# The second token product of a filter-and-mixer kernel in seven products of 256 columns, from the second batch on, with the earlier form of the first batch's filter step

## The chip, the cores and the metric

One core of a Trainium2 chip runs the whole kernel. The time is device microseconds for one execution, as a median of several runs. Before the change it is 2583.15 us (three runs, 2580.81 to 2583.3); the profiled execution has a span of 2581.1 us.

## The reference: what is computed

Eight batches of x (3008 positions, 256 channels, float32) pass two blocks.

```python
X = np.fft.rfft(x, axis=1)                          # gfnet_mixing
x = np.fft.irfft(X * (filt_r + 1j * filt_i), n=3008, axis=1)

h = np.maximum(x.T @ w_tok1, 0.0) @ w_tok2          # token products: 3008 -> 256 -> 3008, per batch
u = x + h.T
h2 = np.maximum(u @ w_ch1, 0.0) @ w_ch2             # channel products: 256 -> 1536 -> 256
out = u + h2
```

The weights arrive as float64, so every piece of them is converted to float32 on the chip once ("conversion" below).

## The kernel before

The Fourier transforms are matrix products with tables. A batch's positions are split as 64 x 47; the first half of the transform is written to DRAM (z_tmp), the middle (32 steps, one for each k) does the second half, the filter and the first half of the inverse, and writes g_tmp; the last half of the inverse is added inside the same PSUM sums as the second token product.

The mixer goes through 8 batches, 6 tiles of 512 positions each (the last 448), and 6 steps `jp` for each tile: 288 items. An item runs the two channel products for a sixth of the hidden width. They are already done in the seven-product form: a 2 x 2 block product with 7 multiplications of 256 columns in place of 8, at the price of sums on VectorE (DVE). The filter of the batches to come runs in between, one or two of its steps for each item.

```python
def u_unit(b, m, h1, ut, dh):            # second token product + last half of the inverse transform
    w = width(m)                         # 512, or 448 for m = 5
    ps = bank(free_bank())
    for t in range(TC):                  # TC = 2
        nc.tensor.matmul(ps[:, 0:w], h1[:, t, ts(dh, P)], w2[:, t, ds(m * 512, w)], start=(t == 0), stop=False)
    for q in range(4):                   # 128 columns each
        ...
        nc.tensor.matmul(ps[:, ds(q * P, n)], t4[b, c][:, r, ts(dh, P)], wai[:, 0:n], start=False, stop=(q == 3))
    nc.scalar.copy(out=ut[:, dh, 0:w], in_=ps[:, 0:w])

def mix(next_ready):
    ...
    for i in range(len(items) + 1):
        ...
        s = up_first(...); up_middle(...)        # 4 of the 7 products; ACT copy, 2 sums on DVE
        one_step()                               # a sum for the next tile, or a part of `finish` of the last one
        for f in h_sums(hhs[i - 1], ...): f()    # 3 sums on DVE
        down(mo, jo, 0, ...)                     # 3 products
        yield b, i % n, 0
        up_last(...)                             # 3 products, 2 sums on DVE, 2 Relus on ACT
        one_step()
        yield b, i % n, 1                        # here the filter's step of the item is put
        down(mo, jo, 1, ...)                     # 4 products
        ...
        if m + 1 < MT and jp in (3, 4):
            u_part(b, m + 1, jp - 3)             # u_unit for the next tile, dh = 0 and 1
        ...
        if b + 1 < B: # four items before the end of a batch
            h1s[b + 1] = token_relu(token_sums(b + 1))
        yield b, i % n, 2
```

Two PSUM banks (`acc`, `b`) serve token sums, `u_unit` and the filter in turn (`free_bank`).

In the first batch the middle of the filter has a form of its own. The tables for the inverse are also kept turned (`turn_i`), so that one DVE instruction makes both products with the real and the imaginary part of the filter:

```python
# before, first batch, each k
nc.vector.tensor_tensor(out=p1, in0=ps.to_broadcast([P, 2, D]), in1=t[:, :, k % KC, :], op=ALU.mult)   # 128 x 512
# two matmuls of 256 columns follow, one with wbs, one with turn_i
```

Beside it 20 of the 28 conversions of token weights are spread over the 32 steps k (`IN_B = 20`); the other 8 follow beside the token sums of the first batch. Four of the sixteen pieces of w_tok2 are joined by TensorE and ACT (`BY_PE = 4`), the others on DVE.

Of the kernel before, what the change touches and what calls it, by code (L numbers as in the profile page):

```python
# [10 lines left out]
FP32 = mybir.dt.float32  # L11
# [3 lines left out]
ALU = mybir.AluOpType  # L15
# [30 lines left out]
PARTS = (0, 64, 112)  # L46
BY_PE = 4
IN_B = 20
EARLY = 12
# [76 lines left out]
def kernel(  # L126
# [24 lines left out]
    g_d = nc.dram_tensor("g_tmp", (B, K2, KR, D), FP32, kind="Internal").ap()  # L151

    def pool(name, bufs, **kw):
        return ctx.enter_context(tc.tile_pool(name=name, bufs=bufs, **kw))
# [38 lines left out]


    filts = [glob.tile([P, 2, KC, D], FP32, name="filt%d" % i) for i in range(FB)]
    w1 = glob.tile([P, A, DT], FP32, name="w1")

    w2 = glob.tile([P, TC, A * P], FP32, name="w2")

    turned = wcp.tile([P, K2 * D + P], FP32, tag="wc", name="turned")  # L200
# [9 lines left out]
    def filt_load(c, first):  # L210
        t, k0 = filts[c % FB], c * KC


        q = nc.gpsimd if first and c != 1 else nc.sync
        for src, i, p0 in ((filt_r, 0, 0), (filt_i, 1, 0 if first else HALF)) + (() if first else ((filt_r, 0, HALF),)):
            q.dma_start(t[p0:p0 + A, i], raw(src, k0, [[64 * D, A], [D, KC], [1, D]]))
            lo = p0 + 32
            if k0 == 0:
                q.dma_start(t[lo:lo + A, i, 0, :], raw(src, 32, [[64 * D, A], [1, D]]))
            k = max(k0, 1)  # L220

            for j0, n in ((0, 16), (16, A - 1 - 16)):
                q.dma_start(t[lo + j0:lo + j0 + n, i, k - k0:KC, :],
                            raw(src, 64 * (j0 + 1) - k, [[64 * D, n], [-D, k0 + KC - k], [1, D]]))

    def filt_double(c):
        t = filts[c % FB]
        nc.scalar.copy(out=t[HALF:P], in_=t[0:HALF])


    turn_i = sp.tile([P, 4, WC, KR], FP32, tag="s", name="turn_i")

    def table_turn(g, wb):
        wi, to = wb[:, :, P:], turn_i[:, g % 4]
        nc.scalar.copy(out=to[0:HALF], in_=wi[HALF:P])
        nc.scalar.activation(out=to[HALF:P], in_=wi[0:HALF], func=AF.Copy, scale=-1.0)

# [10 lines left out]
    def halves(st, n, pair):  # L248

        words = [st.bitcast(t).rearrange("p (n w) -> p n w", w=2)[:, 0:n] for t in (U32, FP32)]  # L250
        lo, hi, hi_f = words[0][:, :, 0], words[0][:, :, 1], words[1][:, :, 1]
        top, rest = (v[:, 0:n] for v in pair)
        top_i, rest_i = top.bitcast(U32), rest.bitcast(U32)


        nc.scalar.activation(out=top, in_=hi_f, func=AF.Copy, scale=2.0 ** -112)  # L256
        yield
        nc.vector.tensor_scalar(out=top_i, in0=top_i, scalar1=3, scalar2=None, op0=ALU.logical_shift_left)
        nc.vector.scalar_tensor_tensor(out=top_i, in0=hi, scalar=0x80000000, in1=top_i,
                                       op0=ALU.bitwise_and, op1=ALU.bitwise_or)  # L260
        yield
        nc.vector.tensor_scalar(out=rest_i, in0=top_i, scalar1=0xFF800000, scalar2=None, op0=ALU.bitwise_and)

        nc.vector.scalar_tensor_tensor(out=rest, in0=lo, scalar=2.0 ** -52, in1=rest, op0=ALU.mult, op1=ALU.mult)
        yield top, rest
# [9 lines left out]
    def rounded(st, n, parts, late):  # L275
        if late:

            pair = (p1p.tile([P, 512], FP32, tag="p1", name="top"), p2p.tile([P, 512], FP32, tag="p2", name="rest"))
        else:
            pair = spare_pair()  # L280
        h = halves(st, n, pair)
        yield next(h)
        yield next(h)
        top, rest = next(h)
        for src, dst in parts:
            nc.vector.tensor_tensor(out=dst, in0=src(top), in1=src(rest), op=ALU.add)
# [17 lines left out]
    def w1_load(i):  # L304
# [14 lines left out]
        yield next(h)  # L319
        yield next(h)  # L320
        on_chip(wai_t, *next(h), 512, [(lambda v: v, w1[:, 2 * i:2 * i + 2, :].rearrange("p a t -> p (a t)"))])

    def w2_load(i):
# [15 lines left out]
        if i < BY_PE:  # L339
            h = halves(st, n + more, spare_pair())  # L340
            yield next(h)
            yield next(h)
            on_chip(ident, *next(h), n + more, parts)
        else:
            yield from rounded(st, n + more, parts, False)
# [23 lines left out]
    def wc2_load(i):  # L369
# [5 lines left out]
        def tile_of(dh):  # L375
# [11 lines left out]
             + [wc1_load(c * (DC // 512), False) for c in range(DH)] + [f(i) for f, i in LAST])  # L387
    begin, copy, middle, end = (iter(tiles) for _ in range(4))

# [9 lines left out]
    def convert():  # L399

        advance(middle)
        convert_end()

    def convert_end():
        ended[0] += 1
# [51 lines left out]
    def dft(bs):  # L457
# [44 lines left out]
        def b_unit(k):  # L502
# [11 lines left out]
            if first:  # L514

                nc.vector.tensor_tensor(out=p1, in0=ps.to_broadcast([P, 2, D]), in1=t[:, :, k % KC, :], op=ALU.mult)
                prods[k] = (p1[:, 0:1], p1[:, 1:2])
                return
            p2 = p2p.tile([P, nb, D], FP32, tag="p2", name="p2")
            prods[k] = (p1,)  # L520
            nc.vector.tensor_tensor(out=p1, in0=ps, in1=fr, op=ALU.mult)
            nc.vector.scalar_tensor_tensor(out=p2[re], in0=ps[im], scalar=-1.0, in1=fi, op0=ALU.mult, op1=ALU.mult)
            nc.vector.tensor_tensor(out=p2[im], in0=ps[re], in1=fi, op=ALU.mult)
            nc.vector.tensor_tensor(out=p1, in0=p1, in1=p2, op=ALU.add)

        def bi_unit(k):
# [4 lines left out]
            for i, p in enumerate(parts):  # L531
                wi = turn_i[:, k // WC % 4, k % WC] if i else wbs[k // WC][:, k % WC, P:]
                nc.tensor.matmul(ps[0:KR], wi, p, start=(i == 0), stop=(i == len(parts) - 1))  # L533
            c, r = divmod(k, KC)
# [17 lines left out]
        if first:  # L552
            filt_double(0)
            table_turn(0, wbs[0])
        for k in range(K2 + 1):
            if k < K2:
# [10 lines left out]
                if first and k % KC == KC - 1 and k + 1 < K2:  # L567
                    filt_double(k // KC + 1)
                    table_turn(k // KC + 1, wbs[k // KC + 1])
            if k >= 1:  # L570
# [19 lines left out]

    def token_relu(acc):
        h1 = h1p.tile([P, TC, D], FP32, tag="h1", name="h1")
# [3 lines left out]
    def width(m):  # L596
        return 512 if m < MT - 1 else 448

    def u_unit(b, m, h1, ut, dh):
# [3 lines left out]
        for t in range(TC):  # L603
            nc.tensor.matmul(ps[:, 0:w], h1[:, t, ts(dh, P)], w2[:, t, ds(m * 512, w)],  # L604
                             start=(t == 0), stop=False)
        for q in range(4):
            c, r = divmod(4 * m + q, TC4)
            n = min(P, w - q * P)
            nc.tensor.matmul(ps[:, ds(q * P, n)], t4[b, c][:, r, ts(dh, P)], wai[:, 0:n],  # L609
                             start=False, stop=(q == 3))  # L610
        nc.scalar.copy(out=ut[:, dh, 0:w], in_=ps[:, 0:w])


# [114 lines left out]

    def u_part(b, m, dh):
        if dh == 0:  # L730
            uts[b, m] = up.tile([P, DH, 512], FP32, tag="u", name="u")
        u_unit(b, m, h1s[b], uts[b, m], dh)

# [16 lines left out]
    def mix(next_ready):  # L750
# [4 lines left out]
        def loads(b):  # L755
            if b + 1 < B and next_ready(b):
                for c in wait:
                    t4_load(b + 1, c)
                wait.clear()

        items = [(b, m, jp) for b in range(B) for m in range(MT) for jp in range(JP)]
        n = MT * JP
        for i in range(len(items) + 1):
# [12 lines left out]
            if old:  # L776
                bo, mo, jo = items[i - 1]
                tts[i - 1] = tp.tile([P, 4, 256], FP32, tag="t", name="t")
                for f in h_sums(hhs[i - 1], tts[i - 1], width(mo)):
                    f()  # L780
                down(mo, jo, 0, hhs[i - 1], tts[i - 1], pos.setdefault((bo, mo), []))
            yield b, i % n, 0
            convert()
# [11 lines left out]
            if now:  # L795
                if m + 1 < MT and jp in (3, 4):
                    u_part(b, m + 1, jp - 3)
                    if jp == 4:
                        wait.append(m + 1)
                        todo_v.extend(v_steps(b, m + 1))  # L800
                if b + 1 < B:
                    j = i % n - n
                    if j == -4:
                        h1s[b + 1] = token_relu(token_sums(b + 1))
                    elif j == -3 or j == -2:
                        u_part(b + 1, 0, j + 3)
                        if j == -2:
                            todo_v.extend(v_steps(b + 1, 0))
            loads(b)
# [4 lines left out]
    with tc.manual_schedule():  # L814
        nc.sync.dma_start(wa0, wa0_d)
        nc.vector.memset(turned[:, A:K2, :], 0.0)
        for t in filts:
            nc.vector.memset(t, 0.0)
        half = 0
        second = dft(GROUPS[1])  # L820
        for i, _ in enumerate(dft(GROUPS[0])):
# [11 lines left out]
            elif k >= 0:  # L833
                while half < 2 * IN_B * (k + 1) // K2:
                    if half % 2:
                        convert_end()
                    else:
                        advance(middle)
                    half += 1

# [12 lines left out]
        chan.extend((both[:, 0], both[:, 1]))  # L853
        for _ in range(XB):
            next(second)
        acc = token_sums(0)
        for _ in range(A // 2 + TC * N2 // NG - IN_B):
            convert()
        h1s[0] = token_relu(acc)
        for dh in range(DH):  # L860
# [60 lines left out]
```

## Time and profile before

| | PE | PE weight loads | DVE | ACT | POOL |
|---|---|---|---|---|---|
| busy us | 2499.2 | 2000.2 | 1795.0 | 708.1 | 530.2 |
| share of the span | 97% | 77% | 70% | 27% | 21% |
| instructions | 10944 | 10944 | 3396 | 1377 | 974 |

In the trace a float32 matmul is two matmul instructions (the down product has 288 items x 7 = 2016 matmuls and 4032 rows of L678), each with its own weight load. Matmul durations overlap each other, so the cost of one in a dense stream is read from the distance between starts and not from its duration. The table is an average over stages. The first 160 us load and convert weights and filter the first batch; from there to about 500 us the mixer of batch 0 shares its time with a dense filter stage for batches 1 and 2; after that one filter step for each item, or none, runs beside the mixer. The chain of work that ended last is 80% PE, 12% DVE, 2% ACT, 2% DMA and 2% issue.

### The profile page before, as it was taken

What the parts mean: (1) busy time and instruction counts of PE and PEld (TensorE: products, weight loads), DVE (VectorE), ACT (ScalarE), POOL (GpSimd) and SP (SyncE); (2) the same over time, 40 slices, a digit from 0 to 9 for tenths busy, and PEclk for the clock granted to TensorE, in tenths of its full rate; (3) what the DMA queues carried; (4) which work ended last, traced back from release to release, by engine and by line L of the source; (5) the groups of instructions that cost most, each with busy time, mean ns of one, the idle gap of its engine ahead of it and who ended that gap; (6) DMA issues with size and microseconds to landing.
All of it is one profiled execution on the core that took longest, in us unless ns stands there. A gap on an engine that the chain in (4) does not pass through costs nothing.

```text
span 2581.1 us, 31406 instructions
## 1 busy us (share of the span) xinstructions
PE 2499.2 (97%) x10944; PEld 2000.2 (77%) x10944; DVE 1795.0 (70%) x3396; ACT 708.1 (27%) x1377; POOL 530.2 (21%) x974
## 2 busy tenths in 40 slices
PE   6789999999999999999999999999999999999998
PEld 3466666888788777887888777788888888888887
DVE  7777878556575888645665888846678577647676
ACT  5623222123221222213321222212222122212222
POOL 5453111111211121112121111211211121211212
PEclk9999999999999999999999999999999999999999
DMA  9964333212332232203332233211332121100001
GB/s 206 248 178 144 108 96 104 92 57 84 96 95 57 83 94 66 80 17 92 96 91 75 75 84 89 80 30 59 89 83 77 50 63 53 25 9 8 17 12 21
DMA packets 153756, 205.20 MB, mean 80 GB/s; under 512 B 34180, under 2 KB 105034, under 8 KB 153598
## 3 DMA queue, kind: packets, MB, share of 16 engines
q1 hardware_dynamic: 82542, 114.27, 15.8%
q0 software_dynamic: 31104, 41.31, 6.7%
q10 hardware_dynamic: 39952, 47.61, 5.8%
q8 instruction: 87, 1.43, 0.2%
q14 instruction: 71, 0.58, 0.1%
HBM read 131.23 MB, written 71.83 MB: 79 GB/s over the span
## 4 chain that ended last, share of the span: by engine, by line
PE 80%; DVE 12%; ACT 2%; issue 2%; DMA 2%; ACTq 0%; POOL 0%; DVEq 0%; SPq 0%; POOLq 0%
PE ps_po L678 28%; PE ps_pg L644 16%; PE ps_pg L660 12%; PE ps_acc L604 4%; PE ps_b L587 3%; PE ps_acc L587 3%; PE ps_b L604 2%; DVE t L622 2%; DVE hh L622 2%; PE ps_acc L533 2%; PE ps_acc L609 2%; PE ps_b L508 1%; PE ps_b L448 1%; DVE u L622 1%; PE ps_acc L508 1%
## 5 line engine op out<-in xcount | busy, mean ns | idle before, releaser
L622 DVE TENSOR_TENSOR hh<-ps_pg,s 128x512 f32<-128x512 f32 (+3 forms) x864 | 482.1, 585 | 608.6 <-ACT s L647 608.1
L723 POOL DMA_DIRECT2D out_dram<-r x757 | 409.8, 550 | 1947.1 <-ACT hh L665 922.2
L665 ACT ACTIVATE hh<-hh 128x512 f32<-128x512 f32 (+1 forms) x576 | 348.0, 621 | 1116.8 <-DVE hh L622 1116.8
L678 PE MATMUL ps_po<-t,wc 128*128 128x256 f32 (+1 forms) x2304 | 535.6, 375 | 6.0 <-DVE t L622 5.1
L678 PEld LDWEIGHTS ps_po<-t,wc 128*128 128x128 f32 x2304 | 434.4, 190 | 131.5 <-issue 52.6
L644 PE MATMUL ps_pg<-v,wc 128*128 128x256 f32 (+1 forms) x1728 | 413.3, 375 | 0.1
L678 PE MATMUL ps_po<-hh,wc 128*128 128x256 f32 (+1 forms) x1728 | 412.8, 375 | 0.2 <-ACT hh L665 0.2
L644 PEld LDWEIGHTS ps_pg<-v,wc 128*128 128x128 f32 x1728 | 326.9, 190 | 40.3 <-DVE v L622 3.0
L678 PEld LDWEIGHTS ps_po<-hh,wc 128*128 128x128 f32 x1728 | 327.6, 190 | 38.6 <-ACT s L647 0.8
L660 PE MATMUL ps_pg<-u,wc 128*128 128x256 f32 (+1 forms) x1152 | 294.5, 378 | 6.2 <-DVE hh L622 5.6
L622 DVE TENSOR_TENSOR t<-t,hh 128x256 f32<-128x256 f32 (+1 forms) x576 | 242.1, 420 | 19.8
L660 PEld LDWEIGHTS ps_pg<-u,wc 128*128 128x128 f32 x1152 | 216.2, 190 | 44.0 <-DVE hh L622 18.9
L622 DVE TENSOR_TENSOR s<-ps_pg,hh 128x512 f32<-128x512 f32 (+1 forms) x288 | 196.1, 681 | 31.1 <-DVE hh L622 1.4
L622 DVE TENSOR_TENSOR t<-hh 128x512 f32<-128x512 f32 (+1 forms) x288 | 192.1, 667 | 0.6 <-ACT hh L665 0.6
L644 PE MATMUL ps_pg<-u,wc 128*128 128x256 f32 (+1 forms) x576 | 169.9, 377 | 1.0 <-DVE hh L622 1.0
L660 PE MATMUL ps_pg<-v,wc 128*128 128x256 f32 (+1 forms) x576 | 169.3, 376 | 0.0
L647 ACT COPY s<-ps_pg 128x256 f32<-128x256 f32 (+1 forms) x288 | 106.0, 368 | 153.6 <-PE ps_pg L644 150.4
L660 PEld LDWEIGHTS ps_pg<-v,wc 128*128 128x128 f32 x576 | 108.8, 190 | 13.5 <-DVE s L622 0.2
L644 PEld LDWEIGHTS ps_pg<-u,wc 128*128 128x128 f32 x576 | 102.7, 191 | 20.7 <-issue 10.5
L604 PE MATMUL ps_acc<-w,h 128*128 128x512 f32 (+1 forms) x228 | 105.6, 585 | 0.7 <-ACT h L593 0.7
L533 PE MATMUL ps_acc<-p,wb 128*96 128x256 f32 (+1 forms) x192 | 80.8, 502 | 17.9 <-ACT t L539 13.3
L587 PE MATMUL ps_b<-t,w 128*128 128x256 f32 x384 | 86.9, 389 | 9.7 <-ACT both L256 8.4
(107 smaller groups left out, 2284.9 us busy)
## 6 DMA issues: line engine op xcount, KB each, us to landing
g_tmp<-t ACTq DMA_DIRECT2D x128, 192.0 KB
out_dram<-r POOLq DMA_DIRECT2D x698, 32.0 KB, 1.8
x<-in_x_dram SPq DMA_DIRECT2D x173, 128.0 KB
z_tmp<-t ACTq DMA_DIRECT2D x84, 256.0 KB
t<-z_tmp SPq DMA_DIRECT2D x112, 192.0 KB
t<-g_tmp SPq DMA_DIRECT2D x42, 512.0 KB
wb<-wbi_t SPq DMA_DIRECT2D x80, 224.0 KB
filt<-in_filt_r_dram SPq DMA_DIRECT2D x129, 48.0 KB
```

What stands on the lines that cost most here:

```text
L508: nc.tensor.matmul(ps, wbs[k // WC][0:P if first else KR, k % WC, 0:P], t2, start=True, stop=True)
L533: nc.tensor.matmul(ps[0:KR], wi, p, start=(i == 0), stop=(i == len(parts) - 1))
L587: nc.tensor.matmul(acc[:, t, :], w1[:, a, ts(t, P)], t4[b, a // TC4][:, a % TC4, :], start=(a == 0 and t == 0), stop=(a == A - 1 and t == ...
L604: nc.tensor.matmul(ps[:, 0:w], h1[:, t, ts(dh, P)], w2[:, t, ds(m * 512, w)], start=(t == 0), stop=False)
L609: nc.tensor.matmul(ps[:, ds(q * P, n)], t4[b, c][:, r, ts(dh, P)], wai[:, 0:n], start=False, stop=(q == 3))
L622: nc.vector.tensor_tensor(out=out, in0=in0, in1=in1, op=op)
L644: nc.tensor.matmul(ps[:, 0:hw], chan[0][:, jp, n, :], mov, start=True, stop=True)
L647: nc.scalar.copy(out=s[:, 0], in_=g[0][:, 0, 0:hw])
L660: nc.tensor.matmul(ps[:, 0:hw], chan[0][:, jp, n, :], mov, start=True, stop=True)
L665: nc.scalar.activation(out=hs, in_=hs, func=AF.Relu)
L678: nc.tensor.matmul(po[i][:, j, 0:hw], chan[1][:, jp, n, :], mov, start=(jp == 0 and first == 1), stop=(jp == JP - 1 and last == 1))
L723: q.dma_start(rows[g, e, :, ds(h * A + 4 * m, n)], blocks[ts(g, CW), h, e, 0:n])
```

## The change

Two things change at once.

**From batch 1 on, the second token product takes the seven-product form too.** For each tile the four matmuls of 512 columns give way to seven of 256. The needed combinations of w_tok2 do not fit on the chip, so POOL forms them once, during batch 0, in the memory of w2 itself, and writes them to DRAM (`w2_tmp`); a tile's seven blocks of 256 columns are read back from there, two tiles ahead, into the memory that w2 has left (`w2m`). The combinations of h1 are formed by POOL for each batch (`combine`). The results leave PSUM by DVE sums in place of ACT copies, in four parts for each tile, over three items. The eight matmuls of 128 columns for the inverse transform stay.

**The first batch's filter goes back to three DVE products for each k**, without the turned tables: one of 128 x 256 and two of 64 x 256. ACT no longer turns tables and doubles only the real part of the filter. Conversions advance by whole rounds, 12 of them beside the 32 steps k and 16 after; six of the pieces of w_tok2 are joined by TensorE (`BY_PE = 6`).

```diff
-BY_PE = 4
-IN_B = 20
+BY_PE = 6
...
+    w2_d = nc.dram_tensor("w2_tmp", (MT, P, 7, 256), FP32, kind="Internal").ap()
+    w2m = [w2[:, t, 0:7 * 256].rearrange("p (s n) -> p s n", s=7) for t in range(2)]
...
-        nc.scalar.copy(out=t[HALF:P], in_=t[0:HALF])
+        nc.scalar.copy(out=t[HALF:P, 0], in_=t[0:HALF, 0])
-    def table_turn(g, wb): ...                        # two ACT instructions for each two k
...
-                nc.vector.tensor_tensor(out=p1, in0=ps.to_broadcast([P, 2, D]), in1=t[:, :, k % KC, :], op=ALU.mult)
-                prods[k] = (p1[:, 0:1], p1[:, 1:2])
-                return
+                p1, p2 = p1[:, 0:1], p1[:, 1:2]
...          # then, as in the other batches:
             nc.vector.tensor_tensor(out=p1, in0=ps, in1=fr, op=ALU.mult)
             nc.vector.scalar_tensor_tensor(out=p2[re], in0=ps[im], scalar=-1.0, in1=fi, ...)
             nc.vector.tensor_tensor(out=p2[im], in0=ps[re], in1=fi, op=ALU.mult)
...
+    def token_relu(b, acc):
+        if b:   # two Relus into the memory of w2, then combine(h1) on POOL
+    def u_quarter(b, m, h1, ut, i):
+        ps = bank(free_bank())
+        if i >= 2:
+            u_filter(b, m, i - 2, ps, True)            # the 4 matmuls of 128 columns
+        todo = (((0, 0), (5, 3)), ((6, 4), (4, 6)), ((1, 1), (2, 2)), ((3, 5),))[i]
+        for j, (n, at) in enumerate(todo):
+            nc.tensor.matmul(ps[:, ds(j * hw, hw)], h1[:, n, :], w2m[m % 2][:, at, 0:hw], ...)
+        if i == 0:
+            nc.scalar.copy(out=c11, in_=p0)
+            v(c22, p1, c11)                            # DVE, 256 columns
+        elif i == 1:
+            v(both, ps[:, 0:w]..., c22...)             # DVE, 512
+            v(c22, p0, c21)                            # DVE, 256
+        else:
+            v(ut[:, i - 2, 0:w], ps[:, 0:w], ut[:, i - 2, 0:w])   # DVE, 512
+    def w2m_load(m):
+        nc.sync.dma_start(w2m[m % 2][:, :, 0:hw], w2_d[m, :, :, 0:hw])
+    def w2_sums(m): ...   # POOL: 2 writes, 2 subtractions, an addition and a subtraction, 2 writes
...
+        own = ({(3, 2): 0, (4, 2): 1}, {(2, 2): 0, (3, 2): 1, (4, 0): 2, (4, 2): 3})   # (jp, place): part
+        new = {(JP - 3, 2): 0, (JP - 2, 0): 1, (JP - 2, 2): 2, (JP - 1, 0): 3}         # tile 0 of the next batch
...
-        for _ in range(A // 2 + TC * N2 // NG - IN_B):
-            convert()
+        for i in range(rounds, A // 2 + TC * N2 // NG):
+            convert()
+            ...
+            if i == A // 2 + BY_PE - 1:
+                sum_up()
+                acc = token_sums(0)
```

## The prediction

> **What bounds the kernel now.** I read the table of engines first: PE is busy for 97% of the span and DVE for 70%. These are averages, so next I cut the trace into stretches of time. Columns: the stretch, its length, then busy us (and instructions) of PE, PE weight loads, DVE, ACT, POOL, then the granted PE clock, the DMA share and GB/s.
>
> ```profile
> 40.00:80.00 40.00, 36.19 (x123) 20.89 (x123) 28.92 (x51) 27.46 (x54) 26.23 (x47) 1.00 0.95 250
> 80.00:120.00 40.00, 31.62 (x110) 19.17 (x109) 25.54 (x51) 24.44 (x49) 20.53 (x37) 0.96 0.88 217
> 120.00:160.00 40.00, 30.91 (x122) 23.81 (x121) 27.69 (x56) 8.16 (x15) 11.35 (x22) 0.87 0.69 164
> ...
> 260.00:310.00 50.00, 46.98 (x186) 33.25 (x185) 40.39 (x72) 11.63 (x23) 1.28 (x3) 1.00 0.33 97
> ...
> 560.00:610.00 50.00, 50.00 (x224) 40.40 (x223) 29.16 (x57) 14.95 (x29) 9.75 (x18) 1.00 0.30 92
> ...
> 910.00:960.00 50.00, 49.96 (x209) 37.55 (x208) 42.09 (x76) 12.89 (x26) 8.68 (x16) 1.00 0.30 83
> ```
>
> Four regimes are to be seen. (a) From 40 to 120 us, the first batch's filter, the DMA engines are full (0.95, 0.88). (b) In batch 0, at 260, PE has gaps and DVE is at 81%: there two filter steps run beside most items. (c) At 560, with the first half of the transform beside the mixer, PE has no gap and DVE is at 58%. (d) At 910, with the middle of the filter beside it, PE still has no gap but DVE is at 84%. From about 500 us on PE alone sets the time. What the new token product saves on PE is thus saved outright, if DVE, which takes over its sums, does not become late in regime (d).
>
> The cost on PE is read from the timeline, as the distance between starts (columns: start us, us, engine and line, operation, how many):
>
> ```profile
> 708.02 1.88 PE L604 MATMUL ps_acc<-w,h 128*128 128x512 f32 x4
> ...
> 709.74 1.05 PE L609 MATMUL ps_acc<-wai,t 128*128 128x128 f32 x8
> ...
> 710.63 0.60 PE L644 MATMUL ps_pg<-u,wc 128*128 128x256 f32 x2
> ...
> 711.07 1.46 PE L644 MATMUL ps_pg<-v,wc 128*128 128x256 f32 x6
> ...
> 712.36 1.46 PE L678 MATMUL ps_po<-hh,wc 128*128 128x256 f32 x6
> ```
>
> Two token matmuls of 512 columns (four rows) take 709.74 - 708.02 = 1.72 us, 0.86 us each. Three of 256 columns take 712.36 - 711.07 = 1.29 us, 0.43 us each: exactly half. The four of 128 columns take 0.89 us.
>
> **What the Trainium skill says.** "TensorE: Matmul & The Clock Gate", section "Back-to-back issue gap", gives the gap of one pass as columns / 2.4 GHz plus some 2.5 ns; for 256 columns and the two rows that this trace has for a float32 matmul the measured 215 ns a row means about 2 x 256 / 2.4, so each row is worth two passes, and the fixed part is too small to make seven short matmuls dear. The section "LDWEIGHTS" puts a weight load at 128 / 1.2 = 107 ns; this trace has 190 ns for it, which still fits under 215 ns. "SBUF — State Buffer", section "Who interferes with whom", says that a DVE instruction with two SBUF inputs contends with a GpSimd instruction that reads SBUF. The trace agrees: while POOL combined the channel weights (120 to 240 us), the conversion's DVE product of 128 x 512 took 760 ns where it takes 692 with POOL quiet.
>
> ```profile
> L264 DVE SCALAR_TENSOR_TENSOR rest<-st,rest 128x512 f32<-128x512 uint32 x10 | 7.6, 760 | 0.3
> L264 DVE SCALAR_TENSOR_TENSOR both<-st,both 128x512 f32<-128x512 uint32 x14 | 9.7, 692 | 0.5
> ```
>
> **Part 1, PE in the token product.** A full tile loses 4 x 0.86 = 3.44 us and gains 7 x 0.43 = 3.01: 0.43 us less. A tile of 448 saves 7/8 of it, 0.38. Batches 1 to 7 have 35 full and 7 short tiles: 35 x 0.43 + 7 x 0.38 = **17.7 us** less. The eight short matmuls stay, 1.78 us a tile. Nothing else on PE goes.
>
> **Part 2, DVE takes over.** Groups by shape (mean ns is the number before the last bar):
>
> ```profile
> L622 DVE TENSOR_TENSOR u<-ps_po,u 128x512 f32<-128x512 f32 x80 | 54.4, 680 | 0.0
> L622 DVE TENSOR_TENSOR u<-ps_po,u 128x256 f32<-128x256 f32 x40 | 16.5, 414 | 0.0
> L611 ACT COPY u<-ps_acc 128x512 f32<-128x512 f32 x48 | 28.1, 586 | 145.7 <-PE ps_acc L609 136.5 <-DMA g_tmp<-t 9.2
> ```
>
> The new sums are of these two shapes: 0.41 in part 0, 0.68 + 0.41 in part 1, 0.68 each in parts 2 and 3, 2.9 us a tile, about 119 us over 42 tiles. ACT, which is no limit, loses two copies of 0.59 and keeps one of 0.37. In regime (d) a tile lasts about 51 us and DVE is busy for 0.84 x 51 = 43 us of it; with 2.9 it comes to 46 in 50.7, 91%. So the sums fit on average, but the slack that DVE had during `u_unit` (4 PE matmuls and 8 short ones without any DVE work) is now broken up, and in the items before it `finish` already makes DVE run late. In the timeline of that regime the filter's last sum ends 2.3 us into the next item's `up_first`, and the sum that `up_last` waits for comes right after it. A part that is put in between adds 0.4 to 1.1 us to DVE there and 0.86 us to PE; only part 1 has more for DVE. Also part 2 and the filter's step behind it use the same PSUM bank, with only 1.29 us of `up_last` between. I estimate 0.3 us lost for each of some 14 tiles in regime (d), and, for the later sums of tile 0 of each batch (its last part now ends one item later, right ahead of its use), 0.3 us for each of 7 batches: **+6 us**.
>
> **Part 3, forming the combinations.** POOL gets six times four sums in batch 0 (some 0.9 us each for 256 columns, twice the 458 ns that L351 takes for 128) and 30 writes, 5.4 MB in all. That stage has DVE at over 80% and PE waiting for it in part, so slowed DVE sums count: 24 sums that each hold up DVE by 0.1 us make **+2 us**. Reading back is 42 loads of 0.92 or 0.80 MB, 37.7 MB over 2080 us, 18 GB/s above some 80 at a DMA share of 0.3 at most, two tiles (100 us) ahead: hidden. The five POOL steps on h1, 0.5 us each, lie beside a whole item: hidden.
>
> **Part 4, the first batch.** DVE before: one instruction of 0.69 us for each k.
>
> ```profile
> L516 DVE TENSOR_TENSOR p<-ps_b,filt 128x512 f32<-128x512 f32 x16 | 11.0, 687 | 7.3 <-ACT filt L228 3.6 <-DMA filt<-in_filt_r_dram 2.1 <-issue 1.4
> L522 DVE SCALAR_TENSOR_TENSOR p<-ps_acc,filt 64x256 f32<-64x256 f32 x16 | 6.8, 426 | 0.4
> L523 DVE TENSOR_TENSOR p<-ps_acc,filt 64x256 f32<-64x256 f32 x16 | 6.7, 418 | 0.2
> ```
>
> After: 0.42 + 0.43 + 0.42 = 1.26 us, over 32 k 18 us more. A conversion costs DVE 2.2 us for w_tok1 (0.42 + 0.69 + 0.42 + 0.69), for w_tok2 1.8 by PE and 2.6 on DVE. Beside the 32 steps it had 22 + 12 x 2.2 + 4 x 1.8 + 4 x 2.6 = 66 us; now 40 + 12 x 2.2 = 67, the same. ACT loses about 20 us there. Eight pieces of w_tok2 (386 KB each, 3.1 MB, 12 us at 250 GB/s) are no longer fetched in the stage that is full of DMA, so it may end some us sooner. But after it DVE has 6 x 1.8 + 10 x 2.6 = 37 us of conversions to do where it had 8 x 2.6 = 21, beside these lines:
>
> ```profile
> 130.81 23.95 PE L587 MATMUL ps_b<-t,w 128*128 128x256 f32 x96 [8.41 <-ACT both L256]
> 154.79 0.60 ACT L593 ACTIVATE h<-ps_b 128x512 f32<-128x512 f32 x1 [15.02 <-PE ps_b L587]
> ```
>
> The filter ended at about 120, the token sums at 154.8: 35 us, in which DVE stood idle for 10. With 37 us and the latency of the first conversion the conversions now end last, 3 or 4 us after the token sums would. Sooner by 0 to 10, later by 3: I take **+1 us**, with +-6 for what I can't read.
>
> **The sum**: 2583 - 17.7 + 6 + 2 + 1 = 2574 us.
>
> **Rivals.** First, *DVE becomes the bound in regime (d)*: 91% on average can mean late in each of the 14 tiles, by up to 1 us, and in batch 0 too, where PE already waits; for it speak the 81 to 88% of DVE with PE gaps at 260 us, against it the full PE at 910 with DVE at 84%. It would make 2585 or more. Second, *the start gets longer*: if the first filter is bound by the chain PE, DVE, PE, ACT of each k rather than by DMA, the extra 0.57 us of each k returns as up to 18 us, and the conversions add theirs; 2590. Against it speaks DMA at 0.95. Third, *the start gets shorter* by what leaves the full DMA stage and ACT: 8 to 10 us, and 2564. Fourth, *the read-back of combinations delays z or g loads* of the filter: the same queue (SP) waits in order for the last part of a tile; but those loads have items of slack and the longest waits from 500 to 2500 us name no DMA that PE waits for. Worth under 2 us.
>
> **Range and chances.** 17.7 us is firm; the deductions can be 2 to 25. Range 2560 to 2590. A change by 2% is 52 us: neither the whole gain nor any rival reaches it. Faster by over 2%: 0.01; within: 0.97; slower: 0.02.
>
> **What the new profile would show.** PE busy down by some 17 us; a tile's seven matmuls spaced by 0.43 us; DVE up by about 135 us; stretches without filter middle (regime c) each shorter by the full 0.43 us a tile; PE waits for DVE sums only in regime (d). The first item of the mixer, at 162.6 us before, between 155 and 170. I am wrong if DVE is above 93% in regime (d) with PE gaps, or if the mixer starts outside these bounds.

## The result, and the profile after

The changed kernel takes **2572.43 us** (median of four runs, 2571.15 to 2574.81); the kernel before, run beside it, 2583.23. The ratio is **0.996, with a 95% interval from 0.9942 to 0.9977**: a small gain, but clear of the noise, and 1.6 us from the 2574 of the prediction. The sum was hit, but not by its terms, as the stretches show. First the token product on PE. This is the timeline of the changed kernel around 700 us, PE alone (start us, us, engine and line, operation, how many):

```profile
695.12 1.03 PE L614 MATMUL ps_acc<-w 128*128 128x256 f32 x4
695.99 1.03 PE L709 MATMUL ps_pg<-u,wc 128*128 128x256 f32 x4
...
700.76 0.60 PE L614 MATMUL ps_acc<-w 128*128 128x256 f32 x2
701.19 0.59 PE L693 MATMUL ps_pg<-u,wc 128*128 128x256 f32 x2
```

L614 is the new product. The first pair is part 2, where two products of 256 columns (four rows) take 695.99 - 695.12 = 0.87 us; the second is part 3, where one takes 701.19 - 700.76 = 0.43. The cost on PE is as predicted. What DVE pays is in the groups by shape (busy us and mean ns ahead of the last bar, idle time after it):

```profile
L671 DVE TENSOR_TENSOR u<-ps_b,u 128x512 f32<-128x512 f32 x54 | 37.3, 691 | 69.4 <-PE ps_b L614 69.4
L671 DVE TENSOR_TENSOR u<-ps_b,u 128x256 f32<-128x256 f32 x39 | 16.5, 424 | 16.3 <-ACT u L620 15.6
```

With the same groups on the other bank and those of the short tile the new sums come to 120.6 us (119 predicted). Now the stretches (length, busy us and instructions of PE, weight loads, DVE, ACT, POOL, then PE clock, DMA share, GB/s), the same as were shown of before:

```profile
40.00:80.00 40.00, 35.34 (x123) 20.98 (x123) 34.52 (x77) 18.56 (x38) 29.24 (x54) 0.96 0.94 243
80.00:120.00 40.00, 39.02 (x123) 20.74 (x124) 35.49 (x78) 21.61 (x42) 16.73 (x31) 1.00 0.90 242
120.00:160.00 40.00, 34.53 (x140) 25.70 (x139) 36.91 (x74) 11.91 (x21) 19.13 (x34) 0.96 0.60 174
...
260.00:310.00 50.00, 46.35 (x181) 32.38 (x180) 43.86 (x78) 12.63 (x25) 9.54 (x17) 1.00 0.40 114
...
560.00:610.00 50.00, 50.00 (x233) 42.10 (x232) 32.30 (x61) 14.19 (x29) 8.67 (x16) 1.00 0.37 115
...
910.00:960.00 50.00, 49.74 (x215) 38.73 (x214) 45.13 (x81) 12.06 (x24) 6.42 (x13) 1.00 0.36 106
```

At 910 us DVE stands at 45.13 of 50, 90% (84% before, 91% predicted), and PE now misses 0.26 us where it missed 0.04. Over the whole of tile 1 of batch 2 it is 47.3 of 52.3 us, 91%, where it was 44.3 of 52.2, 85%. In the whole run DVE's busy time grew by 148.7 us (135 predicted). The big difference is at the top: at 80 to 120 us PE has 39.0 us of work where it had 31.6. The first batch is done much sooner. Three lines of the timeline answer to the start shown of before:

```profile
120.55 20.88 PE L570 MATMUL ps_b<-t,w 128*128 128x256 f32 x96
...
141.47 0.60 ACT L582 ACTIVATE h<-ps_b 128x512 f32<-128x512 f32 x1
...
153.94 0.59 PE L693 MATMUL ps_pg<-u,wc 128*128 128x256 f32 x2
```

The token sums of the first batch begin at 120.55 in place of 130.81 and the mixer's first item at 153.94 in place of 162.57: **8.6 us** won at the start in this pair of traces. From there to the last matmul (2557.58 after, 2570.82 before) the token product wins only 13.2 - 8.6 = **4.6 us** of the 17.7. What follows the last matmul takes 1.5 us longer, so the span falls by 11.7 us, from 2581.1 to 2569.4. Up to the issue of the last store that part is as long as before (7.2 us); the 1.5 us lie behind it. From the last matmul to the end all kernels with the new token product take 11.6 to 12.2 us, those without it 10.2 to 10.8. Why is not shown.

Where 13 us of the 17.7 stay is seen by taking, for each tile but the last of the 48, the distance from its first item to the next tile's, after minus before. Where no middle of the filter runs beside it a tile is mostly shorter by 0.41 to 0.46 us (0.35 to 0.37 where the product is that of a short tile), the whole saving. The others:

| tiles (counted from 0) | after minus before, us | lost against -0.41, about us in all |
|---|---|---|
| beside the filter's middle: tiles 1 to 3 of batches 2 and 4 | +0.06 to +0.09, one -0.24 | 2.6 |
| the same: tiles 3 and 4 of batch 5, tile 1 of batch 6 | +0.39, +0.42, +0.40 | 2.4 |
| first tiles of batches 2, 4, 6 | +0.64, +0.64, +1.02 | 3.6 |
| last tiles of batches 1, 3, 5 | +0.06, +0.05, +0.20 | 1.6 |
| tile 4 of batch 2 (no filter's middle) | +1.01 | 1.4 |
| tiles 0 to 4 of batch 0 (the old product) | sum +1.3, of it tile 0 +0.95 | 1.3 |

In tile 4 of batch 2 the issue of two stores of the filter (L529) holds ACT for 2.19 us and so the copy behind it, for which DVE and then PE wait; in e2 the same two take 0.81 us and the tile is 0.31 us shorter than before. Seven of the eleven kernels with the new token product show the long issue, e11 among them, the three without it do not. All eleven issue a load of combinations (0.9 MB) 6.7 us ahead of this tile; whether it is the reason is not shown. Tile 0 of batch 0 is taken up under e1 and e2.

Three waits that the kernel before doesn't have name the first four rows. First two rows, shown at tile 1 of batch 2 (timeline of the changed kernel, all engines; PEld is PE's weight load, a bracket gives the idle time before and what ended it):

```profile
896.85 0.70 DVE L759 STREAM_TRANSPOSE r<-u 128x512 f32<-128x512 f32 x1
...
898.45 1.02 PE L518 MATMUL ps_acc<-p,wb 128*96 128x512 f32 x2
...
898.96 1.28 DVE L671 TENSOR_TENSOR hh<-ps_pg,s 128x512 f32<-128x512 f32 x2
...
899.67 1.23 ACT L714 ACTIVATE hh<-hh 128x512 f32<-128x512 f32 x2 [4.81 <-DVE hh L671]
...
900.80 0.56 ACT L524 COPY t<-ps_acc 96x512 f32<-96x512 f32 x1
901.42 0.73 PEld L614 LDWEIGHTS ps_acc<-w 128*128 128x128 f32 x4 [0.62 <-ACT t L524]
901.42 1.13 PE L614 MATMUL ps_acc<-w 128*128 128x256 f32 x4 [0.22 <-ACT t L524]
```

Read upwards: part 0 (L614) wants the bank `acc`, which the filter's step has until ACT has copied it out (L524). That copy stands on ACT behind two Relus (L714), those wait for DVE's sums (L671), and DVE is late because it has just done a transpose of the tile before (L759). The Trainium skill, "PSUM — Partial Sum Buffer", section "Engine vs sequencer instructions", says that the queues of ScalarE (ACT), VectorE and GpSimd are strictly first in, first out; these lines agree: what the copy of 0.56 us reads was there at 899.47 (898.45 + 1.02, L518), ahead of the Relus' start at 899.67, and the copy started behind them at 900.80. Third row, the first item of batch 2: its second product waits for the sum `v`, which DVE makes once the late part 3 is there.

```profile
825.73 0.88 DVE L671 TENSOR_TENSOR v<-v,u 128x256 f32<-128x256 f32 x2
826.20 1.16 PEld L693 LDWEIGHTS ps_pg<-v,wc 128*128 128x128 f32 x6 [1.27 <-DVE v L671]
```

Fourth row, the last tile of batch 1: a filter step (L494) waits for a bank until DVE has emptied part 1 of tile 0 of batch 2.

```profile
811.34 1.10 PE L494 MATMUL ps_b<-t,wb 96*128 96x512 f32 x2 [0.23 <-DVE u L671]
```

### The profile page after: what moved, and what is told of

Read it like the earlier page. It is cut to its first block, busy times and chain, and to the rows that moved or that the text cites. A ratio compares the mean times of both kernels' runs of the same rounds, so it can differ in the third digit from the quotient of the medians.

```text
span 2569.4 us, 32318 instructions
## 1 busy us (share of the span) xinstructions
PE 2490.2 (97%) x11204; PEld 2048.2 (80%) x11204; DVE 1943.7 (76%) x3668; ACT 660.0 (26%) x1312; POOL 577.2 (22%) x1051
## 4 chain that ended last, share of the span: by engine, by line
PE 71%; DVE 17%; DMA 3%; issue 2%; ACT 2%; SPq 1%; ACTq 0%; DVEq 0%; POOL 0%; POOLq 0%
PE ps_po L727 25%; PE ps_pg L693 15%; PE ps_pg L709 10%; DVE t L671 3%; PE ps_acc L570 3%; DVE hh L671 3%; PE ps_b L614 2%; PE ps_b L570 2%; PE ps_acc L614 2%; DVE u L671 2%; DVE s L671 2%; PE ps_acc L592 2%; PE ps_b L592 2%; PE ps_acc L434 1%; PE ps_acc L518 1%
## 5 line engine op out<-in xcount | busy, mean ns | idle before, releaser
L671 DVE TENSOR_TENSOR hh<-ps_pg,s 128x512 f32<-128x512 f32 (+3 forms) x864 | 482.5, 586 | 283.8 <-ACT s L696 273.6
L714 ACT ACTIVATE hh<-hh 128x512 f32<-128x512 f32 (+1 forms) x576 | 347.9, 621 | 1180.1 <-DVE hh L671 1180.1
L671 DVE TENSOR_TENSOR t<-t,hh 128x256 f32<-128x256 f32 (+1 forms) x576 | 244.5, 424 | 19.8
L709 PEld LDWEIGHTS ps_pg<-u,wc 128*128 128x128 f32 x1152 | 216.1, 190 | 41.9 <-DVE hh L671 15.7
L671 DVE TENSOR_TENSOR s<-ps_pg,hh 128x512 f32<-128x512 f32 (+1 forms) x288 | 196.0, 681 | 31.1 <-PE ps_pg L693 0.8
L671 DVE TENSOR_TENSOR t<-hh 128x512 f32<-128x512 f32 (+1 forms) x288 | 193.2, 671 | 0.6 <-ACT hh L714 0.6
L671 DVE TENSOR_TENSOR u<-ps_b,u 128x512 f32<-128x512 f32 (+3 forms) x111 | 63.4, 571 | 99.6 <-PE ps_b L614 81.1
L671 DVE TENSOR_TENSOR u<-ps_acc,u 128x512 f32<-128x512 f32 (+3 forms) x99 | 57.3, 579 | 95.5 <-PE ps_acc L614 79.3
L693 PEld LDWEIGHTS ps_pg<-u,wc 128*128 128x128 f32 x576 | 109.6, 191 | 23.1 <-issue 10.7
L518 PE MATMUL ps_acc<-p,wb 128*96 128x256 f32 (+1 forms) x256 | 96.0, 475 | 11.6 <-DVE p L510 4.3
```

Of the source, the lines that this page charges most:

```text
L518: nc.tensor.matmul(ps[0:KR], wbs[k // WC][:, k % WC, P:], p, start=(i == 0), stop=(i == len(parts) - 1))
L671: nc.vector.tensor_tensor(out=out, in0=in0, in1=in1, op=op)
L693: nc.tensor.matmul(ps[:, 0:hw], chan[0][:, jp, n, :], mov, start=True, stop=True)
L709: nc.tensor.matmul(ps[:, 0:hw], chan[0][:, jp, n, :], mov, start=True, stop=True)
L714: nc.scalar.activation(out=hs, in_=hs, func=AF.Relu)
```

## The experiments

Differences of tiles are always against the kernel before. The mixer's start is only good to some 3 us: kernels with the same first 150 us began it between 153.7 and 157.0. e3, e5 to e8, e10 and e12 were timed once, and the 21 times of e1 spread over 6.5 us; so for these kernels the tiles and waits are read, and totals only where they differ by more.

**e1 and e2: the two halves apart.** e1 is the kernel before with only the first batch's older form; e2 is the changed kernel with the first batch as in the kernel before.

```diff
 # e1, on the kernel before
-BY_PE = 4, IN_B = 20, table_turn, one product of 128 x 512 for each k
+BY_PE = 6, 12 rounds beside the filter, three products for each k
 # e2, on the kernel before
-u_unit for all batches
+token_relu, u_quarter, w2_sums, w2m_load from batch 1 on
```

> The old first-batch form alone (three filter products for each k, 12 conversions beside them, 16 after), the token product as before. Theory A (the start is what got shorter): the mixer's first matmul comes at 154 +-1.5 us as in the changed kernel, against 162.6, and the whole is 7 to 9 us shorter than before, about 2575 us. Theory B (the start's gain is only borrowed: the mixer of batch 0, bound by DVE and the second filter stage, gives it back): the mixer starts early, but the token sums of batch 1 come at about 490 us as before and the whole stays at 2581 to 2584. Prediction on record: +1 us.

> The token product in seven products alone, the first batch as in the kernel before. Theory A (two independent parts): the mixer starts at 162.6, the whole is 3 to 5 us shorter than before, 2578 to 2580 us, and the tile times from batch 1 on equal those of the changed kernel within 0.1 us. Theory B (token product as predicted, the trace comparison hides it): 9 to 10 us shorter. Sum of this run's gain and that of the start alone: 11 to 13 us.

e1: 2578.4 us, ratio 0.9982 (0.9975 to 0.9988); mixer's start 155.9. e2: 2578.66 us, ratio 0.9983 (0.9974 to 0.9992); mixer's start 163.7, and its tiles from batch 1 on differ from before as in the changed kernel, batch 0 hardly at all. So the two parts bring 5.4 and 5.1 us of the 10.8 and add up. In e2 batch 0, where POOL forms the combinations, costs nothing. Tile 0 of batch 0 is +1.27 in e1, and over the eight kernels with the older form it goes from -0.56 to +3.91: it takes up the spread of the start. Counted to the end of that tile these eight are 4.5 to 9.4 us ahead of the kernel before, the changed kernel 7.7 of its 8.6; the 5.4 us of e1's median are the better measure of the start.

**e3: part 0 half an item later.** If only PE's place for part 0 is bad, another place cures it.

```diff
-own[True] = {(2, 2): 0, (3, 2): 1, (4, 0): 2, (4, 2): 3}
+own[True] = {(3, 0): 0, (3, 2): 1, (4, 0): 2, (4, 2): 3}
```

> Only the place of part 0 moves, from the end of the third item of a tile to the middle of the fourth. Theory (PSUM bank: part 0 waits for the ACT copy of the filter's inverse product, which stands behind two Relus that a late DVE holds up): the wait of TensorE on that copy goes, tiles beside the middle of the filter get 0.5 us shorter (0.9 us in batches 5 and 6), about 6 to 8 us in the whole against the changed kernel, 2564 to 2567 us. Rival (DVE has too much work in this stage): the lost time only moves to another item, tile times change by less than 0.15 us.

2571.7 us: no gain in batches 2 and 4, whose tiles mostly stay at +0.07 (one -0.24, one +0.39); about 2.4 us in batches 5 and 6, which tile 0 of batch 0 (+3.91) hides in the total. In batch 2 the wait had only changed its owner. The waits of e3 for batch 2 (who waited <- for whom: us in all, times, longest):

```profile
PEld ps_acc L494 <- DVE u L671: 2.3, 4, 0.6
```

and those of the changed kernel in the same batch:

```profile
PEld ps_acc L614 <- ACT t L524: 2.4, 4, 0.6
```

Now the filter's step behind part 0 waits for the bank until DVE has emptied part 0. Four waits of up to 0.6 us either way: there the order of PE was not the cause.

**e4 and e9: the third and fourth rows of the table.** Tile 0's parts of the next batch are put at the same early places as the others, and the token sums with their Relus an item earlier. In e4 those Relus overwrite the last of w2 before its combinations are formed, so a part of its output is computed from other numbers, with the same work; e9 has POOL's writing an item earlier, which mends this, and computes all.

```diff
 # e4, on e3
-new = {(JP - 3, 2): 0, (JP - 2, 0): 1, (JP - 2, 2): 2, (JP - 1, 0): 3}
+new = {(3, 0): 0, (3, 2): 1, (4, 0): 2, (4, 2): 3}
-if b + 1 < B and i % n == n - 4:      # token sums of the next batch
+if b + 1 < B and i % n == n - 5:
 # e9, on e4
-if i >= 8 and to_dram:
+if i >= 7 and to_dram:
```

> As the run with part 0 moved, and also tile 0 of the next batch: token sums one item earlier, its four parts at the places of the other tiles, so that its sums are done a full item before their use. Theory: besides the bank wait, the first item of batches 2, 4 and 6 loses the 0.9 to 1.1 us for which its second product waited for the sums, and the last tile of batches 1, 3 and 5 the 0.5 us for which a filter step waited for a bank: 4 to 5 us more than part 0 alone, 2560 to 2563 us, ratio to before 0.991 to 0.992. Rival: the earlier token sums wait for their t4 loads, and nothing is won or some us lost.

> The places of e4 (own parts (3,0), (3,2), (4,0), (4,2); tile 0 of the next batch at the same places of tile 5; token sums five items before the end of a batch), with one difference: POOL's six writings of the combinations in batch 0 start one item earlier, so that all of them are done before the Relus of batch 1 use the memory of w2. Theory (the waits of tile 0 and of the last tile come only from the places of the parts): 2565 us as in e4, ratio 0.993, first tiles of batches 2, 4, 6 at -0.1 to -0.45 us against the kernel before and the last tiles of batches 1, 3, 5 at -0.5 to -0.6. Rival (e4 was fast in part because its writings and reads fell together in another way): 2570 to 2573.

e4: 2564.87 us, ratio 0.9931 (0.9919 to 0.9944). e9: **2566.13 us, ratio 0.9932 (0.9918 to 0.9946)**. In e9 the first tiles of batches 2, 4, 6 are at -0.08, -0.09, -0.39 and the last tiles of 1, 3, 5 at -0.56, -0.56, -0.52. Some 5 us of the loss were thus a matter of places, or of the token sums that moved with them. Tiles 1 to 3 of batches 2 and 4 stay at +0.08, but for one (-0.22).

**e8: without DVE's part sums.** Parts 0 to 3 leave PSUM by ACT copies and the sums that join them are left out, so the output lacks them.

```diff
-v(c22, p1, c11)                                # likewise the other sums of u_quarter
+nc.scalar.copy(out=c22, in_=p1)
```

> The changed kernel with the four parts leaving PSUM by ACT copies, without their DVE sums: the second token product's sums are left out, so the output is not the reference's. DVE has 2.9 us a tile less. Theory (part 0 waits for its bank because of the order on ACT): tiles beside the middle of the filter keep at least 0.35 of the 0.5 us that they lose. Rival (too much work for DVE): those tiles get 0.4 us or more shorter, as the tiles without the filter's middle did, and the first items of batches 2, 4 and 6 lose their 1.1 us of waiting.

2572.49 us. Tiles 1 to 3 of batch 2 are at +0.07, +0.75, +0.10, the four waits of part 0 still at 2.4 us. This was against what I thought: the sums that the change gave to DVE are not what makes DVE late. They come from the end of item 2 on, DVE's lateness is in items 0 to 2. (The copies load ACT in DVE's place, but they too come behind the waits of part 0.) Over tile 1 of batch 2 DVE is busy for 44.5 of 52.3 us here, 85% as before the change. Only the last tiles of batches 1, 3, 5 got their 0.4 us back.

**e10 and e12: without the transposes.** The finishing steps of the tile before (sums and two transposes) lie in items 0 to 2. POOL copies of the same size take the transposes' place; the transposing is left out, so what is stored is in another order. e12 does the same to the kernel before.

```diff
-nc.vector.transpose(r[:, 0:w // CW, dh, :], ut[:, dh, 0:w]...)
+nc.gpsimd.tensor_copy(out=r[:, 0:w // CW, dh, :], in_=ut[:, dh, 0:w]...)
```

> The changed kernel with the two DVE transposes of each tile (703 ns each, inside the finishing steps of the tile before) replaced by POOL copies of the same size; the transposing is left out, so what it stores is in another order than the reference's. DVE has 1.4 us less to do in items 0 to 2 of each tile. Theory (in the regime with the middle of the filter DVE is late in items 0 to 2 because of the finishing steps, so ACT's Relus and the filter's copy behind them are late, and part 0 waits for that bank): tiles 13 to 16 and 25 to 28 fall from 52.27 to 51.8 us or below and the 0.6 us waits of the first rows of part 0 for the filter's ACT copy are gone; about 2570. Rival (the copy is late for another reason, the order of PE and ACT alone): tiles stay at 52.2 to 52.3, the waits stay. Not told apart from a lighter DVE: POOL's copies may slow DVE sums by some per cent.

> The kernel before with the same replacement as e10 (two DVE transposes of each tile replaced by POOL copies, so the output's order isn't the reference's). A control: how much of e10's gain is not the change's own. Theory: in batches 2 to 6 the kernel before loses nothing to DVE there, so its tiles stay as they are (within 0.1 us) and only batch 0, where its PE has gaps, gets shorter, by 1 to 4 us: 2579 to 2582. Rival (the kernel before too pays for late DVE there): tiles 13 to 16 fall by some 0.5 us, 2573 or less; then e10 does not explain what the change lost.

e10: 2559.06 us, a larger gain than I expected. Tiles 1 to 3 of batches 2 and 4 are at -0.43, -0.23, -0.40 and -0.72, -0.41, -0.40, and the waits of part 0 are gone. The same place as above, in e10's timeline:

```profile
894.33 1.23 ACT L714 ACTIVATE hh<-hh 128x512 f32<-128x512 f32 x2 [4.22 <-DVE hh L671]
...
895.46 0.56 ACT L524 COPY t<-ps_acc 96x512 f32<-96x512 f32 x1
...
896.08 0.83 PEld L614 LDWEIGHTS ps_acc<-w 128*128 128x128 f32 x4
```

Against the filter's matmuls of the same item (L518, last one at 893.70 here and at 898.45 there) ACT's copy starts 1.76 us later here, 2.35 us later there: 0.6 us, and no bracket follows L614. In e12 (2579.5 us beside 2584.2) those tiles of the kernel before move by +0.29, -0.01, +0.01 and -0.31, 0.00, +0.02; only batch 0 (1.1 us each in tiles 2 and 3) and the last tiles of batches 1, 3, 5 (0.5 each) gain. The kernel before has the same late copy in the same item:

```profile
907.56 1.02 PE L533 MATMUL ps_b<-p,wb 128*96 128x512 f32 x2
...
908.79 1.23 ACT L665 ACTIVATE hh<-hh 128x512 f32<-128x512 f32 x2 [4.81 <-DVE hh L622]
...
909.92 0.56 ACT L539 COPY t<-ps_b 96x512 f32<-96x512 f32 x1
```

It starts 2.36 us after the filter's matmuls, and over items 0 to 2 of that tile DVE is busy for 22.96 of 23.67 us, while no wait of PE is seen in these tiles. So it had the same late DVE and paid nothing for it, because nothing on PE wanted that bank so early.

**e11: less DVE in the finishing steps, with all work kept.** On e9, three of those sums that read SBUF alone go to POOL.

```diff
-v(us[:, 0, 0], us[:, 0, 0], p1)
-v(us[:, 0, 1], us[:, 0, 1], u2)
-v(us[:, 1], us[:, 1], u3...)
+nc.gpsimd.tensor_tensor(...)            # the same three
```

> e9 with three of the finishing sums that read SBUF alone moved from DVE to POOL: two of 128 x 256 (0.75 us together on DVE) and one of 128 x 512 (0.68 us). Nothing is left out. DVE has 1.4 us less to do in items 1 and 2 of each tile, as in e10, POOL about 3.6 us more. Theory (the half microsecond of each tile with the middle of the filter is lost because DVE is late from the finishing steps): tiles 13 to 15 and 25 to 27 at -0.3 to -0.45 us against the kernel before where e9 has +0.09; with the same in batches 0, 5 and 6 some 6 to 10 us less than e9: 2556 to 2560. Rival (POOL's sums of 0.9 to 1.8 us come too late for the transposes that follow them on DVE, or slow DVE's own sums by reading SBUF beside them): no gain, 2566 or more, and waits of DVE's transposes for POOL.

**2559.87 us, ratio 0.9907 (0.989 to 0.9923)**: the fastest of all that do the whole work, 12.6 us below the changed kernel. Tiles 1 to 3 of batches 2 and 4 are at -0.31, -0.50, -0.48 and -0.81, -0.50, -0.41. Of the 7.8 us between the profiled executions of e9 and e11 2.4 lie in the start, whose spread is as large. In the stretch at 910 us PE has no gap again:

```profile
910.00:960.00 50.00, 49.95 (x216) 38.95 (x215) 45.63 (x79) 13.03 (x25) 11.34 (x19) 1.00 0.35 103
```

Tile 1 of batch 4 has DVE busy for 46.8 of 51.7 us, 90.5%; in the changed kernel it was 47.3 of 52.3, 90.6%. So e11 with the same load loses nothing there, and e8 with 85% loses as much as the changed kernel: it is not DVE's average that costs, but what it does in three of the six items.

**e5, e6, e7: the start.** Two things changed beside the filter's 32 steps, the form of the product and the number of conversions (20 became 12). e5 is the changed kernel with the one-instruction product and ACT's turned tables, but 12 conversions; e6 with three products, but 20 conversions; e7 the changed kernel with eight copies of 385 KB from DRAM to DRAM beside the filter, for the pieces of w_tok2 that the change moved out of it.

```diff
 # e5
+nc.vector.tensor_tensor(out=p1, in0=ps.to_broadcast([P, 2, D]), in1=t[:, :, k % KC, :], op=ALU.mult)
+table_turn(...)
 # e6
-(k + 1) * (A // 2) // K2 > k * (A // 2) // K2
+(k + 1) * 20 // K2 > k * 20 // K2
 # e7
+if k % 3 == 0 and k < 24: nc.sync.dma_start(junk_d[...], x[B - 1, ...])
```

> The changed kernel with one thing of the start undone: the first batch makes both filter products in one DVE instruction from turned tables again (ACT turns them and doubles both filter parts); 12 conversions beside the filter and 16 after stay. Theory A (the start got shorter because 8 pieces of w_tok2 left the stage that is full of DMA): mixer start stays at 154 +-1.5 us or comes earlier. Theory B (it got shorter because ACT was relieved of turning and doubling, some 20 us): mixer start goes back to 160 to 163 us.

> The changed kernel with 20 conversions beside the first filter and 8 after it, three filter products for each k. Theory A (DMA-full stage): the filter ends later by about 12 us (118 in place of 106), what is saved after it does not make up for it, mixer start 159 to 166 us. Theory B (ACT relief): the filter ends at 106 to 110 us, and the mixer starts at or before 154. DVE also has about 19 us more to do beside the filter here, so a late end alone does not prove A.

> The changed kernel with eight extra copies of 385 KB, DRAM to DRAM, spread over the first filter's steps; nothing reads them, so the result stays. They put back the 3.1 MB that the change took out of this stage, without any work on an engine. Theory A (DMA-full stage): the filter ends 8 to 13 us later (114 to 119 in place of 106) and the mixer starts that much later. Theory B (ACT relief): it ends within 3 us of 106.

The end of the last filter step of the first batch, in us:

| | 12 conversions beside it | 20 conversions |
|---|---|---|
| three products | 106.0 (changed kernel), 110.2 with e7's copies | 120.1 (e6) |
| one product, turned tables | 116.2 (e5) | 120.7 (before), 122.7 (e2) |

The eight kernels of the first cell's form lie between 106.0 and 108.1, three of the last cell's between 120.1 and 122.7. So both were needed: one product with 12 conversions gains 4.5 us, three products with 20 nothing beyond the spread, both together 14.7. What e7's copies cost there, 2 to 4 us, is little more than the spread. e5 ran 2579.76 us (its mixer starts at 164.2), e7 2580.1 (163.6: behind the filter PE waits 4.0 us for x, which the copies delay). e6 ran 2596.81 (177.4), but its start after the filter is not comparable: there a filter step of batch 1 stands on PE behind the token sums, and its copy on ACT holds up conversions behind it for 31 us; only its filter's end is read here.

What the older form gains at 12 conversions, though it has three DVE instructions for one, is in the timeline of e5:

```profile
64.59 1.04 ACT L230 COPY filt<-filt 64x1024 f32<-64x1024 f32 x1
...
65.66 0.35 ACT L237 COPY turn_i<-wb 64x192 f32<-64x192 f32 x1
...
66.02 0.36 ACT L238 ACTIVATE turn_i<-wb 64x192 f32<-64x192 f32 x1
66.40 0.37 ACT L533 COPY t<-ps_acc 96x256 f32<-96x256 f32 x1
...
66.82 0.67 PE L527 MATMUL ps_acc<-p,wb 128*96 128x256 f32 x2 [1.73 <-ACT t L533]
```

The copy that frees the one bank of the inverse (L533) stands on ACT behind the doubling of the filter, now of both parts, and two turns, and PE waits 1.73 us. The waits from 30 to 118 us, of e5:

```profile
PEld ps_acc L527 <- ACT t L533: 24.7, 22, 7.1
PE ps_acc L527 <- ACT t L533: 15.7, 7, 6.7
```

and of the changed kernel:

```profile
PEld ps_acc L518 <- ACT t L524: 13.5, 20, 3.9
PE ps_acc L518 <- ACT t L524: 3.4, 1, 3.4
```

That is 12 us less in which PE waits for ACT. Neither engine nor DMA is full in e5 (DVE 41.5 of the 75 us from 30 to 105, ACT 41.9, DMA share 0.80), so these waits point to the order on ACT, not to a load. e5 puts the one product and ACT's turns back together, so no run shows it for ACT's turns alone. In e6 the limit is another: DVE is busy for 67.7 of 75 us and DMA at 0.93, and from these I can't tell which of the two sets it.

## Why the prediction was right or wrong

**Part 1 (-17.7 us on PE): right.** 0.43 us for each product, and 0.41 to 0.46 us for each full tile that nothing disturbs. PE's busy time fell by only 9.0 us (2499.2 to 2490.2), not the 17 that I gave as a sign: the sum of durations overlaps and is no measure of it, the distances between starts are.

**Part 2 (DVE takes over, +6 us): the term was mis-sized, about 10 us, and half its mechanism was wrong.** The 14 tiles of 0.3 us (4 us) were nine, all but one of 0.5 to 0.8, 5.0 us in all. Tile 0 of each batch, taken at 7 x 0.3, cost 3.6 us in three batches and nothing in the others. The last tiles of batches 1, 3, 5 (1.6 us) were in no term. The mechanism was right in one half: `finish` makes DVE late, and a bank carries that to PE. It was wrong in the other, that the new sums break DVE's slack: in the tiles beside the filter's middle e8 has none of them and loses the same. What the change added to the critical path there was an early claim of part 0 on a bank (e3 moves the wait, e10 and e11 take it away). And the load of DVE, 91% as predicted, said nothing of it: e11 has as much and loses nothing.

**Part 3 (forming the combinations, +2 us): too much.** Batch 0 in e2 is as long as before. Reading back cost nothing that a wait of PE names; only the 1.4 us in tile 4 of batch 2 may come from it. The writes were 24, not 30. And the 760 ns from which DVE's slowing was read mix two cases: in the trace of before five of those ten products met POOL's work and took 825 to 831 ns, the other five 692 or 693.

**Part 4 (the start, +1 us): wrong, -8.6 us in the traces, -5.4 in e1's median; the third rival held.** I set the filter's end at 0 to 10 us sooner; it was 14.7. The step that failed is the comparison of DVE's work before and after (66 and 67 us, "the same"): in the kernel before DVE was busy for 51 of the 75 us from 30 to 105, in the changed one for 66, so DVE had been waiting and its sum could not decide. The 20 us that ACT loses I named and gave no value (ACT was busy for 61 to 69% of the stage); e5's waits show that ACT held the bank. The conversions after the filter cost more than the 3 us I gave: from the filter's end to the mixer it is 48 us in place of 42. My bounds for the mixer's start, 155 to 170, did not hold (153.9).

**The sum** came within 2 us by luck, because errors cancel: in the traces about 10 us better at the start, against about 5 us worse in the tiles and 1.5 us behind the last store's issue. Of the rivals, the first (DVE the bound beside the filter's middle) is half true: time was lost there, but by order and not by load. The second (a longer start) did not show. Of the fourth (the read-back delays loads) no wait of PE shows anything; the long issue of two stores in tile 4 of batch 2 stays open.

## What to carry to other kernels

When a step on the full engine is moved to an earlier place, ask which bank or buffer it claims there, who must free it, and what stands ahead of that one in its engine's order: an ACT copy of 0.56 us behind two Relus behind a late DVE cost half a microsecond a tile, with ACT busy for a quarter of the time. Summing an engine's work tells whether a stage fits, not how long it takes; look first at whether that engine waits in the stage now. And where an engine is late in some items only, move work of those items (e11's three sums), not the new work.

## What was not expected of the hardware

Taking two transposes of 701 ns (1.4 us of DVE work a tile) from DVE brought some 0.5 us for most of the disturbed tiles, and moving three sums of 1.4 us together to POOL about the same, though DVE's busy time in a tile fell by only 0.6 us with the sums (47.3 to 46.8). On POOL they take 2.7 us (groups of e11), where I had estimated 3.6:

```profile
L755 POOL TENSOR_TENSOR u<-u,r 128x512 f32<-128x512 f32 x40 | 50.8, 1269 | 0.0
...
L752 POOL TENSOR_TENSOR u<-u,r 128x256 f32<-128x256 f32 x40 | 29.0, 726 | 22.4 <-DVE u L671 22.4
```

That POOL works beside DVE for 5 us more at 910 to 960 us (11.34 in e11, 6.38 in e9) did not undo it.
